# A recurrence step whose first product is cut into column halves of TensorE's array, with part of it summed in the second product's bank

## Chip, cores and metric

The kernel runs on one core of a Trainium2 chip. The metric is the device time of one execution in microseconds (us), the median of several runs. A core has five engines that take their own instructions in order: TensorE (PE; its weight loads are listed as PEld), VectorE (DVE), ScalarE (ACT), GpSimd (POOL) and SyncE (SP, which here issues most DMA transfers). TensorE writes only to PSUM, which has eight banks; GpSimd doesn't read PSUM here.

## What is computed

Two parts. The first is a recurrence over 768 tokens for 4 x 8 heads with a state of 40 x 40 each; the second sends its output through a layer of eight experts. All in f32.

```python
for t in range(S):                                   # S = 768, D = 40
    y[:, :, t] = einsum('bhd,bhde->bhe', rt, state)
    Sa = einsum('bhde,bhe->bhd', state, at)
    state = state * wt[:, :, None, :] - einsum('bhd,bhe->bhde', Sa, bt) \
            + einsum('bhd,bhe->bhde', vt, kt)
...
P = softmax-like weights of x @ w_gate               # x: 3072 x 320, normalised 8 times over rows and columns
for e in range(E):                                   # E = 8, F = 1024
    out += P[:, e:e+1] * (np.maximum(x @ w1[e], 0) @ w2[e])
```

## The kernel before

The recurrence is cut into 12 chunks of 64 tokens (c). In a chunk the tokens' effects on each other are products of small matrices and one triangular inverse, so that only the state goes from chunk to chunk. The 32 heads are four batches (b) of four pairs (p = 0 to 3) of two heads (h = 0, 1). Head 0 of a pair lies on rows 0 to 39, head 1 on rows 64 to 103 of a tile, so a tile has R2 = 104 rows. One step is one (c, b): 48 steps in all.

- `prep(c, b)` makes a step's matrices ahead of it: running products of w (q, g by DVE), scaled k, b and a (kb, ab, mostly by POOL), and from products of those the weights `sx` (104 rows; for each p and h 104 columns: 64 for the chunk's own tokens, then 40 that carry the state and k) and `bb`. It stores g in DRAM (gd).
- `load_lu`, `inv_...`, `finish`, `tload` and `tmat` make the triangular inverses of a group of two chunks and put them together as `tt`; tmat's products are gp (L261) and op (L266), with 64 rows and 64 columns of weights each. gp's operands lie on rows 0 to 63, op's on rows 64 to 127.
- `recur(c, b)` is the step. It loads vz, rb, gl and f, then: av (L289) from r and the state, masked by DVE into f (L290); the first product `xc` (L297), 104 columns of weights from sx times f, one bank for each h; from each bank ACT copies rows 0 to 63 to x1 (L303) and rows 64 to 103 to c1 (L304); pu = tt times x1 (L308), masked by DVE to pm (L310); the second product c2 = bb times pm (L315); DVE adds c1 to it (ws, L317); POOL multiplies columns 0 to 63 by gl to the output y (L321), and columns 64 to 103 by cc to the next state z (L330; in chunks 9 to 10 DVE does that). z is transposed on TensorE (zt, L335) and copied by ACT into vz (L337, L338) and into the next f (L285, L286).
- Every second step stores y to DRAM (xd) and queues a small product lp (`gate`, L345), which `gate_step` hands out one matmul at a time between those of xc.

The four batches are staggered (SKEW) by the list of events at the end of `attention`. That is the order in which the code issues work. The order on each engine is then set by the language's scheduler from its own model of time, up to the eighth block of the experts (N_MAN); behind that it is as written. So a change in one step moves instructions of the whole recurrence on all engines. PSUM tiles of a step come from a pool of four banks (`ps`) that are taken in turn; f has three buffers, gl two, y two, z four.

The experts' part loads and splits weights (`prep_w`) and tokens (`prep_x`), and runs layer1 (L582) and layer2 (L647) with fp32r operands in blocks. Its first blocks are issued behind the recurrence, and the scheduler lets some of their matmuls in between the last steps.

A matmul is given a part of TensorE's 128x128 array by its shape: with 64 columns of weights or fewer half of the array's columns, with 64 rows or fewer half of its rows. Which half follows from the rows on which the output or the operands lie.

Of the kernel before, what the change touches and what calls it, by code (L numbers as in the profile page):

```python
# [11 lines left out]
F32 = mybir.dt.float32  # L12
F32R = mybir.dt.float32r
AF = mybir.ActivationFunctionType
ALU = mybir.AluOpType
# [4 lines left out]
NCH = S // C  # L20
NP = 4
R2 = 104
# [7 lines left out]
def attention(ctx, tc, d, xd, ps, pq, pt, gs, lg):  # L30
    nc = tc.nc
# [3 lines left out]
    const = ctx.enter_context(tc.tile_pool(name="a_const", bufs=1))  # L35
    io = ctx.enter_context(tc.tile_pool(name="a_io", bufs=1))
    wk = ctx.enter_context(tc.tile_pool(name="a_wk", bufs=2))
# [13 lines left out]
    for n in range(NCH * NB - NSX, NCH * NB):  # L51
        i, pool = n % NSX, sets[n - NCH * NB + NSX]
# [12 lines left out]
    lg_b = [const.tile([128, 4 * NP, 64], F32, name="lg")]  # L65
    ab_b = [pin.tile([R2, NP, 128], F32, name=f"ab{i}") for i in range(2)]
    g1_b = [pin.tile([RL, NP, 65], F32, name=f"g1{i}") for i in range(1)]
    vz_b = [const.tile([RL, NP, 104], F32, name=f"vz{i}") for i in range(5)]
    c1_b = [const.tile([R2, NP, 104], F32, name=f"c1{i}") for i in range(2)]
    rb_b = [const.tile([RL, NP, 128], F32, name=f"rb{i}") for i in range(NRB)]  # L70
    y_b = [const.tile([RL, NP, 2, 64], F32, name=f"y{i}") for i in range(2)]
    unf = inv.tile([128, 1056], F32, name="un")
# [14 lines left out]
    def clear():  # L87
        nc.gpsimd.memset(unf, 0.0)
        nc.gpsimd.memset(unf[:, 0:1024:33], 1.0)
        nc.gpsimd.memset(tnf, 0.0)  # L90
        for t in vz_b + rb_b + c1_b + lg_b:
            nc.vector.memset(t, 0.0)
        for t in y_b:
            nc.gpsimd.memset(t[96:RL], 0.0)
        for t in tt_b:
            nc.gpsimd.memset(t, 0.0)
# [6 lines left out]
            nc.scalar.copy(out=sx_b[i][64:R2].rearrange("r p h x -> r (p h) x")[:, :, 64:104],  # L103
                           in_=cst[64:R2, 360:400].unsqueeze(1).broadcast_to([40, 8, 40]))

    state = {"sx": 0, "ab": 0, "g1": 0, "vz": 0, "c1": 0, "t1": 0, "tt": 0, "rb": 0, "y": 0}

    def rot(key, lst):
        i = state[key]
        state[key] = (i + 1) % len(lst)  # L110
        return lst[i]
# [158 lines left out]
    def recur(c, b):  # L270
        pp = preps[c, b]
        vz, zc = vz_cur[b], zp[b]
        nc.sync.dma_start(out=vz[:, :, 0:64], in_=d["v"][c, b])
        rb = rot("rb", rb_b)
        for h in range(2):
            nc.sync.dma_start(out=rb[h * 64:h * 64 + 48, :, h * 64:h * 64 + 64], in_=d["r"][c, b, h])
        gl = io.tile([RL, NP, 65], F32, name="gl", bufs=2)
        nc.sync.dma_start(out=gl.rearrange("r p t -> r (p t)"), in_=pp["g"][:, 0:260])
        f = wk.tile([R2, NP, 2, 104], F32, name="f", bufs=NFB)
        nc.sync.dma_start(out=f[0:64].rearrange("s p h x -> s (p h) x")[:, :, 64:104],  # L280
                          in_=d["vt"][c, b].rearrange("s (g x) -> s g x", x=40))
# [6 lines left out]
        for p in range(NP):  # L288
            nc.tensor.matmul(av[:, p], lhsT=vz[0:R2, p], rhs=rb[0:R2, p], start=True, stop=True)  # L289
        nc.vector.tensor_tensor(  # L290
            out=f[:, :, :, 0:64], in0=av,
            in1=mask_f.unsqueeze(1).unsqueeze(1).broadcast_to([R2, NP, 2, 64]), op=ALU.mult)
        yield
        xc = [ps.tile([R2, NP, 104], F32, name=f"xc{h}", tag="ps") for h in range(2)]
        for h in range(2):
            for p in range(NP):
                nc.tensor.matmul(xc[h][:, p], lhsT=pp["sx"][:, p, h], rhs=f[:, p, h], start=True, stop=True)  # L297
                if p % 2:
                    gate_step()
        x1 = wk.tile([128, NP, 104], F32, name="x1")  # L300
        c1 = rot("c1", c1_b)
        for h in range(2):
            nc.scalar.copy(out=x1[h * 64:h * 64 + 64], in_=xc[h][0:64])  # L303
            nc.scalar.copy(out=c1[h * 64:h * 64 + 40], in_=xc[h][64:104])  # L304
        yield
        pu = ps.tile([128, NP, 104], F32, name="pu", tag="ps")
        for p in range(NP):
            nc.tensor.matmul(pu[:, p], lhsT=tts[c][:, b * NP + p], rhs=x1[:, p], start=True, stop=True)  # L308
        pm = wk.tile([128, NP, 104], F32, name="pm")
        nc.vector.tensor_tensor(out=pm, in0=pu, in1=mask_p.unsqueeze(1).broadcast_to([128, NP, 104]),  # L310
                                op=ALU.mult)
        yield
        c2 = ps.tile([R2, NP, 104], F32, name="c2", tag="ps")
        for p in range(NP):
            nc.tensor.matmul(c2[:, p], lhsT=pp["bb"][:, p], rhs=pm[:, p], start=True, stop=True)  # L315
        ws = wk.tile([R2, NP, 104], F32, name="ws")
        nc.vector.tensor_tensor(out=ws, in0=c2, in1=c1, op=ALU.add)  # L317
        if b % 2 == 0:
            ys[c, b // 2] = rot("y", y_b)
        y = ys[c, b // 2]  # L320
        nc.gpsimd.tensor_tensor(out=y[0:R2, :, b % 2], in0=ws[:, :, 0:64], in1=gl[0:R2, :, 0:64], op=ALU.mult)  # L321
        if b % 2:
            tok = c * 256 + b // 2 * 128
            nc.sync.dma_start(out=xd[0:NP * RL].rearrange("(r p) t -> r p t", p=NP)[:, :, tok:tok + 128],
                              in_=y.rearrange("r p b t -> r p (b t)"))
            gq.append(gate(c, b, y))
        if c + 1 == NCH:
            return
        z = wk.tile([R2, NP, 40], F32, name="z", bufs=4)
        (nc.vector if c >= 9 else nc.gpsimd).tensor_tensor(out=z, in0=ws[:, :, 64:104],  # L330
                                in1=preps[c + 1, b]["cc"].unsqueeze(2).broadcast_to([R2, NP, 40]), op=ALU.mult)
        yield
        zt = ps.tile([40, NP, 104], F32, name="zt", tag="ps")
        for p in range(NP):
# [1 line left out]
        vz = rot("vz", vz_b)  # L336
# [15 lines left out]
    def gate_step():  # L352
        if len(gq) > (GL - 1) // 2:
            next(gq[0])
            gcount[0] += 1
            if gcount[0] % NP == 0:
                gq.popleft()
# [4 lines left out]
    preps, invs, tts = {}, {}, {}  # L362
# [23 lines left out]
    def step(c, b):  # L386
        if (c, b) not in gens:
            gens[c, b] = recur(c, b)
        next(gens[c, b], None)
# [6 lines left out]
    for c in range(NCH):  # L396
# [3 lines left out]
        t = 5 * c + 2 - T_LEAD  # L400
# [3 lines left out]
    for s, cs in enumerate(GROUPS):  # L404
# [3 lines left out]
        for i in range(n):  # L408
            cb = (cs[0] + i // NB, i % NB)
            j = cb[0] * NB + cb[1] - NSX  # L410
            t = 5 * (j // 4) + 3 + SKEW * (j % 4) + 0.01
            t = max(t, t0 + P0[s] + PD * i) if s else -20 + 0.01 * i
# [53 lines left out]
def body(ctx, tc, d, out):  # L466
# [12 lines left out]
    with ExitStack() as actx:  # L479
        ps, pq, pt = (actx.enter_context(tc.tile_pool(name=f"a_ps{i}", bufs=n, space=bass.MemoryType.PSUM))  # L480
                      for i, n in enumerate((PC, PQ, PT)))
        nc.sync.dma_start(out=gs, in_=d["gate"])
        attention(actx, tc, d, xd, ps, pq, pt, gs, lg)
        nc.gpsimd.memset(ones, 1.0)
        nc.sync.dma_start(out=ident, in_=d["cst"][:, 232:360])
# [350 lines left out]
```

## Time and profile before

| | us |
|---|---|
| median of 3 runs | 1834.67 (1831.1 to 1841.27) |
| the profiled execution's own time | 1832.94 |
| its span in the trace | 1831.2 |
| mean granted TensorE clock | 0.959 |

The trace comes from one execution. "Line engine op, out<-in" names a group of instructions by the code's line and the program's tiles; "x" is the count of records. An f32 matmul in the code leaves two records each of weight load and matmul (a transpose leaves one). "Idle before" is time in which the engine stood still ahead of an instruction, with what ended it. In the view by time a matmul's duration contains its way through the array and overlaps the next one, so the pace is read from start to start. "<-" in a view of waits reads: this waited for that.

### The profile page before, as it was taken

The numbers are of one execution on the slowest core, as the hardware profiler recorded it, in microseconds if no ns is written. First come the engines' busy times: TensorE is split into PE (matmuls) and PEld (weight loads), VectorE is DVE, ScalarE is ACT, GpSimd is POOL, SyncE is SP. The second block draws the span as 40 slices with busy tenths as digits, with TensorE's granted clock in tenths as the row PEclk, the third lists the DMA queues.
The fourth block names the chain that finished last, engine by engine and source line by source line (L and its number), as shares of the span: only waits on it lengthen the run. The fifth ranks groups of instructions, "written<-read, shape, count | busy, mean of one in ns | idle before, by whom it ended". The sixth has DMA issues, their size and how long they took to land.

```text
span 1831.2 us, 31655 instructions
## 1 busy us (share of the span) xinstructions
PE 1724.3 (94%) x11843; PEld 1696.8 (93%) x11843; DVE 1365.3 (75%) x2356; ACT 856.8 (47%) x1851; POOL 874.0 (48%) x854
## 2 busy tenths in 40 slices
PE   4479988999989999999999999999999999999999
PEld 4368888898978999999999999999999999999999
DVE  7786996973788867777676878977686877767675
ACT  6347767766743533434343434345343343424342
POOL 6545664723462626447291735008182644628160
PEclk8568988999999999999999999999999999999999
DMA  7468777867520101111020112201020111102001
GB/s 193 116 157 185 175 180 174 186 137 172 152 77 20 57 20 57 38 39 57 20 75 20 57 37 61 69 1 60 16 76 20 57 38 38 57 20 75 15 24 44
DMA packets 211759, 140.47 MB, mean 77 GB/s; under 512 B 162965, under 2 KB 193813, under 8 KB 211605
## 3 DMA queue, kind: packets, MB, share of 16 engines
q1 hardware_dynamic: 207925, 132.70, 27.9%
q10 hardware_dynamic: 3680, 5.74, 1.2%
q8 instruction: 94, 1.54, 0.3%
q14 instruction: 60, 0.49, 0.1%
HBM read 110.78 MB, written 27.61 MB: 76 GB/s over the span
## 4 chain that ended last, share of the span: by engine, by line
PE 75%; DVE 7%; DMA 4%; issue 4%; POOL 3%; ACT 2%; SPq 2%; POOLq 0%; ACTq 0%; DVEq 0%
PE op L647 36%; PE p L582 33%; DMA inp<-in_inp_dram 1%; PE xc L297 1%; PE av L289 1%; PE pu L308 1%; DVE pr L193 1%; DVE hl L606 1%; DVE q L124 1%; PE c L315 1%; DMA ld<-lt 1%; PE op L266 1%; DVE sm L600 1%; PE ll L159 1%; POOL ab L154 1%
## 5 line engine op out<-in xcount | busy, mean ns | idle before, releaser
L582 PE MATMUL p<-xch,wh 128*128 128x384 f32 (+1 forms) x1792 | 605.0, 339 | 8.9 <-DVE sm L600 4.3
L603 ACT ACTIVATE hh<-sm 128x384 fp32r<-128x384 f32 x512 | 269.5, 527 | 728.5 <-DVE sm L600 728.4
L647 PE MATMUL op<-wh,hh 128*128 128x320 f32 x1536 | 477.2, 311 | 4.0 <-ACT hh L603 3.8
L647 PE MATMUL op<-wl,hh 128*128 128x320 f32 x1536 | 474.8, 310 | 0.0
L647 PE MATMUL op<-wh,hl 128*128 128x320 f32 x1536 | 468.0, 309 | 0.9 <-DVE hl L606 0.9
L528 POOL TENSOR_TENSOR wl<-ws,wh 128x640 fp32r<-128x640 f32 x60 | 103.1, 1718 | 606.2 <-ACT wh L526 606.1
L606 DVE SCALAR_TENSOR_TENSOR hl<-sm,hh 128x384 fp32r<-128x384 f32 x512 | 373.1, 762 | 2.6 <-ACT hh L603 1.8
L582 PEld LDWEIGHTS p<-xch,wh 128*128 128x128 f32 (+1 forms) x1792 | 337.0, 188 | 13.3 <-DVE sm L600 5.2
L582 PE MATMUL p<-xcl,wh 128*128 128x384 f32 x896 | 302.3, 337 | 0.0
L582 PE MATMUL p<-xch,wl 128*128 128x384 f32 x896 | 301.8, 337 | 0.0
L647 PEld LDWEIGHTS op<-wh,hh 128*128 128x128 f32 x1536 | 290.2, 189 | 4.9 <-ACT hh L603 4.9
L647 PEld LDWEIGHTS op<-wl,hh 128*128 128x128 f32 x1536 | 291.1, 190 | 0.0
L647 PEld LDWEIGHTS op<-wh,hl 128*128 128x128 f32 x1536 | 286.8, 188 | 1.4 <-DVE hl L606 1.2
L600 DVE TENSOR_TENSOR sm<-p,u 128x384 f32<-128x384 f32 x384 | 236.3, 625 | 8.7
L582 PEld LDWEIGHTS p<-xcl,wh 128*128 128x128 f32 x896 | 168.6, 188 | 0.0
L582 PEld LDWEIGHTS p<-xch,wl 128*128 128x128 f32 x896 | 168.5, 188 | 0.0
L600 DVE TENSOR_TENSOR sm<-p,p 128x384 f32<-128x384 f32 x128 | 71.3, 557 | 129.4 <-PE p L582 75.0
L600 DVE TENSOR_TENSOR p<-p,p 128x384 f32<-128x384 f32 x128 | 71.1, 556 | 101.7 <-PE p L582 101.4
L600 DVE TENSOR_TENSOR u<-p,p 128x384 f32<-128x384 f32 x128 | 70.8, 553 | 57.1 <-PE p L582 55.9
L536 POOL TENSOR_TENSOR wl<-ss,wh 128x512 fp32r<-128x512 f32 x60 | 90.3, 1505 | 28.4 <-ACT wh L533 24.2
L159 PE MATMUL ll<-ab,kb 104*128 104x128 f32 x336 | 62.8, 344 | 40.5 <-POOL kb L147 18.5
L159 PEld LDWEIGHTS ll<-ab,kb 104*128 104x128 f32 x336 | 54.2, 244 | 45.3 <-POOL kb L147 24.8
(163 smaller groups left out, 2727.3 us busy)
## 6 DMA issues: line engine op xcount, KB each, us to landing
ws<-in_wts_dram SPq DMA_DIRECT2D x60, 832.0 KB, 4.5
inp<-in_inp_dram SPq DMA_DIRECT2D x42, 451.5 KB, 4.5
gd<-g SPq DMA_DIRECT2D x48, 113.8 KB, 2.6
gl<-gd SPq DMA_DIRECT2D x48, 113.8 KB, 2.8
vz<-in_v_dram SPq DMA_DIRECT2D x48, 112.0 KB, 3.5
xd<-y SPq DMA_DIRECT2D x24, 224.0 KB, 3.5
ld<-lt ACTq DMA_DIRECT2D x40, 128.0 KB, 2.6
rb<-in_r_dram SPq DMA_DIRECT2D x96, 48.0 KB, 3.1
```

The lines of the kernel that those rows point to most:

```text
L124: nc.vector.tensor_tensor_scan(out=qr.rearrange("r p t -> r (p t)"), data0=w65[:, 260:0:-1], data1=one65, initial=0.0, op0=ALU.mult, op1=A ...
L154: eng.tensor_tensor(out=ab[64:104, :, 64:128], in0=a_in[64:104], in1=g[64:104], op=ALU.mult)
L159: nc.tensor.matmul(ll[:, p], lhsT=kb[:, p], rhs=ab[:, p], start=True, stop=True)
L193: nc.vector.tensor_tensor(out=prv, in0=a.unsqueeze(2).broadcast_to([nu, n_c, n_r, n_k]), in1=m.unsqueeze(1).broadcast_to([nu, n_c, n_r, n_ ...
L266: nc.tensor.matmul(op[:, p], lhsT=gs[:, p], rhs=t2[:, p], start=True, stop=True)
L528: g.tensor_tensor(out=wl[:, 0:640], in0=raw[:, 256:896], in1=wh[:, 0:640], op=ALU.subtract)
L536: g.tensor_tensor(out=lv[:, 3:7], in0=so[:, :, 0], in1=hv[:, 3:7, 0], op=ALU.subtract)
L582: nc.tensor.matmul(o, lhsT=w_, rhs=x_, start=(j == 0), stop=(j == 3))
L600: eng.tensor_tensor(out=out, in0=x, in1=y, op=ALU.add)
L603: nc.scalar.activation(out=hh[:, f, h], in_=sm[f][:, h], func=AF.Relu)
L606: v.scalar_tensor_tensor(out=hl[:, f, h], in0=sm[f][:, h], scalar=0.0, in1=hh[:, f, h], op0=ALU.max, op1=ALU.subtract)
L647: nc.tensor.matmul(ops[i], lhsT=a[:, h, cs], rhs=w_[:, cw], start=(f == 0 and h == 0 and j == 0), stop=(last and h == 1 and j == 2))
```

## The change

The first product no longer uses 104 columns of weights. Its 64 columns go to `xc` alone, head 0 to rows 0 to 63 and head 1 to rows 64 to 127 of one bank, which one ACT copy takes to x1. The 40 columns are separate matmuls that open the sums of the second product's bank: head 0 with a slice of 64 columns that begins at the 40 (the 24 columns behind them land on rows that nothing uses), head 1 with 40. The second product then adds to the same bank, so c1 and ws go. DVE multiplies z and y out of the bank, z first; POOL does neither any more.

```diff
-        xc = [ps.tile([R2, NP, 104], F32, name=f"xc{h}", tag="ps") for h in range(2)]
-        for h in range(2):
-            for p in range(NP):
-                nc.tensor.matmul(xc[h][:, p], lhsT=pp["sx"][:, p, h], rhs=f[:, p, h], start=True, stop=True)
-                if p % 2:
-                    gate_step()
+        xc = ps.tile([128, NP, 104], F32, name="xc", tag="ps")
+        sf = pp["sx"].rearrange("r p h x -> r p (h x)")
+        for p in range(NP):
+            for h in range(2):
+                nc.tensor.matmul(xc[h * 64:h * 64 + 64, p], lhsT=sf[:, p, h * 104:h * 104 + 64], rhs=f[:, p, h],
+                                 start=True, stop=True)
+            gate_step()
         x1 = wk.tile([128, NP, 104], F32, name="x1")
-        c1 = rot("c1", c1_b)
-        for h in range(2):
-            nc.scalar.copy(out=x1[h * 64:h * 64 + 64], in_=xc[h][0:64])
-            nc.scalar.copy(out=c1[h * 64:h * 64 + 40], in_=xc[h][64:104])
+        nc.scalar.copy(out=x1, in_=xc)
...
         for p in range(NP):
-            nc.tensor.matmul(c2[:, p], lhsT=pp["bb"][:, p], rhs=pm[:, p], start=True, stop=True)
-        ws = wk.tile([R2, NP, 104], F32, name="ws")
-        nc.vector.tensor_tensor(out=ws, in0=c2, in1=c1, op=ALU.add)
+            nc.tensor.matmul(c2[0:64, p], lhsT=sf[:, p, 64:128], rhs=f[:, p, 0],
+                             start=(p == 0), stop=False, skip_group_check=True)
+            nc.tensor.matmul(c2[64:104, p], lhsT=sf[:, p, 168:208], rhs=f[:, p, 1],
+                             start=(p == 0), stop=False, skip_group_check=True)
+        for p in range(NP):
+            nc.tensor.matmul(c2[:, p], lhsT=pp["bb"][:, p], rhs=pm[:, p], start=False, stop=True,
+                             skip_group_check=True)
+        if c + 1 < NCH:
+            z = wk.tile([R2, NP, 40], F32, name="z", bufs=4)
+            nc.vector.tensor_tensor(out=z, in0=c2[:, :, 64:104],
+                                    in1=preps[c + 1, b]["cc"].unsqueeze(2).broadcast_to([R2, NP, 40]), op=ALU.mult)
...
-        nc.gpsimd.tensor_tensor(out=y[0:R2, :, b % 2], in0=ws[:, :, 0:64], in1=gl[0:R2, :, 0:64], op=ALU.mult)
+        nc.vector.tensor_tensor(out=y[0:R2, :, b % 2], in0=c2[:, :, 0:64], in1=gl[0:R2, :, 0:64], op=ALU.mult)
...
-        z = wk.tile([R2, NP, 40], F32, name="z", bufs=4)
-        (nc.vector if c >= 9 else nc.gpsimd).tensor_tensor(out=z, in0=ws[:, :, 64:104],
-                                in1=preps[c + 1, b]["cc"].unsqueeze(2).broadcast_to([R2, NP, 40]), op=ALU.mult)
```

The two c1 buffers and their clearing go too. In the rows that follow, "x4" counts matmuls of the code, each of which is two records in the trace; the sizes are output rows and columns. TensorE, one step after the preparations have ended, before:

```order
L335 MATMUL zt<-cst,z 40x104 x4
L315 MATMUL c_4594<-pm,st_185 104x104 x4
L308 MATMUL pu<-x_4545,tt_217 128x104 x4
L297 MATMUL xc_4611<-f,st_187 104x104 x2
L266 MATMUL op<-td,lg 64x32 x8
L297 MATMUL xc_4611<-f,st_187 104x104 x2
L297 MATMUL xc_4612<-f,st_187 104x104 x4
L289 MATMUL av<-rb_232,vz_224 104x128 x4
```

The same place after (the lines have other numbers there: L312 and L314 are the 40 columns, L317 the second product):

```order
L337 MATMUL zt<-cst,z 40x104 x4
L312 MATMUL c_4646<-f,st_185 64x104
L314 MATMUL c_4646<-f,st_185 40x104
L312 MATMUL c_4646<-f,st_185 64x104
L314 MATMUL c_4646<-f,st_185 40x104
L312 MATMUL c_4646<-f,st_185 64x104
L314 MATMUL c_4646<-f,st_185 40x104
L312 MATMUL c_4646<-f,st_185 64x104
L314 MATMUL c_4646<-f,st_185 40x104
L317 MATMUL c_4646<-pm,st_185 104x104 x4
L305 MATMUL pu<-x_4600,tt_217 128x104 x3
L265 MATMUL op<-td,lg 64x32 x8
```

The eight new matmuls stand right ahead of the second product of the same step, behind zt, in alternating halves of the array; op moves from between xc's matmuls to between pu's. On DVE, in the same stretch before:

```order
L310 TENSOR_TENSOR pm<-pu,cst 128x416
L290 TENSOR_TENSOR f<-av,cst 104x8x64
L317 TENSOR_TENSOR ws<-c_4878,c_229 104x416
L330 TENSOR_TENSOR z<-ws,cc_195 104x160
L310 TENSOR_TENSOR pm<-pu,cst 128x416
L290 TENSOR_TENSOR f<-av,cst 104x8x64
```

And after (L321 is z, L326 y, L307 pm, L289 f):

```order
L321 TENSOR_TENSOR z<-c_4702,st_190 104x160
L326 TENSOR_TENSOR y_231<-c_4702,gl 104x4x64
L307 TENSOR_TENSOR pm<-pu,cst 128x416
L351 COPY lg<-lp 128x8
L289 TENSOR_TENSOR f<-av,cst 104x8x64
L321 TENSOR_TENSOR z<-c_4797,st_191 104x160
L326 TENSOR_TENSOR y_232<-c_4797,gl 104x4x64
L307 TENSOR_TENSOR pm<-pu,cst 128x416
```

z and y stand where ws stood, and the next step's pm and f are queued behind y. At the end of the recurrence, TensorE before, with the experts' first matmuls (p, L582) ahead of the last second product:

```order
L308 MATMUL pu<-x_5523,tt_218 128x104 x4
L582 MATMUL p_5786<-xch_5628,wh_5630 128x384
L582 MATMUL p_5786<-xcl_5629,wh_5630 128x384
L582 MATMUL p_5786<-xch_5628,wl_5631 128x384
L582 MATMUL p_5786<-xch_5628,wh_5630 128x384
L582 MATMUL p_5794<-xch_5628,wh_5630 128x384
L582 MATMUL p_5794<-xcl_5629,wh_5630 128x384
L582 MATMUL p_5794<-xch_5628,wl_5631 128x384
L582 MATMUL p_5794<-xch_5628,wh_5630 128x384
L315 MATMUL c_5543<-pm,bb_215 104x104 x4
```

And after:

```order
L347 MATMUL lp<-gs,y_231 128x8
L584 MATMUL p_5827<-xch_5720,wh_5722 128x384
L584 MATMUL p_5827<-xcl_5721,wh_5722 128x384
L584 MATMUL p_5827<-xch_5720,wl_5723 128x384
L584 MATMUL p_5827<-xch_5720,wh_5722 128x384
L584 MATMUL p_5841<-xch_5720,wh_5722 128x384
L584 MATMUL p_5841<-xcl_5721,wh_5722 128x384
L584 MATMUL p_5841<-xch_5720,wl_5723 128x384
L584 MATMUL p_5841<-xch_5720,wh_5722 128x384
L317 MATMUL c_5629<-pm,bb_215 104x104 x4
```

These eight are the only ones of the experts ahead of the last second product after the change; before, twenty more stand between the last four steps.

More of the change, by code (lines that the diff above doesn't have):

```diff
@@ L68, in attention @@
     vz_b = [const.tile([RL, NP, 104], F32, name=f"vz{i}") for i in range(5)]
-    c1_b = [const.tile([R2, NP, 104], F32, name=f"c1{i}") for i in range(2)]
     rb_b = [const.tile([RL, NP, 128], F32, name=f"rb{i}") for i in range(NRB)]
@@ L90, in clear @@
         nc.gpsimd.memset(tnf, 0.0)
-        for t in vz_b + rb_b + c1_b + lg_b:
+        for t in vz_b + rb_b + lg_b:
             nc.vector.memset(t, 0.0)
@@ L104, in first_use @@
                            in_=cst[64:R2, 360:400].unsqueeze(1).broadcast_to([40, 8, 40]))
-    state = {"sx": 0, "ab": 0, "g1": 0, "vz": 0, "c1": 0, "t1": 0, "tt": 0, "rb": 0, "y": 0}
+    state = {"sx": 0, "ab": 0, "g1": 0, "vz": 0, "t1": 0, "tt": 0, "rb": 0, "y": 0}
     def rot(key, lst):
```

## The prediction

> **What bounds the kernel now.** I read the page's busy times first, then the busy time by stage, then TensorE's instructions in order of time, its waits, and last the groups of the other engines. The page's first line of engines and the stages:
>
> ```profile
> PE 1724.3 (94%) x11843; PEld 1696.8 (93%) x11843; DVE 1365.3 (75%) x2356; ACT 856.8 (47%) x1851; POOL 874.0 (48%) x854
> 100.00:384.00 284.00, 251.75 (x2316) 240.94 (x2317) 223.34 (x398) 193.25 (x488) 156.83 (x184) 0.89 0.79 176
> 384.00:484.00 100.00, 95.72 (x945) 91.32 (x943) 61.92 (x108) 67.73 (x162) 35.19 (x42) 0.95 0.70 160
> 484.00:505.00 21.00, 20.43 (x178) 19.79 (x178) 13.91 (x27) 12.51 (x28) 8.45 (x11) 1.00 0.37 110
> 505.00:570.00 65.00, 55.51 (x320) 51.93 (x318) 55.03 (x91) 26.62 (x52) 37.13 (x34) 0.95 0.17 55
> 570.00:1831.00 1261.00, 1253.12 (x7866) 1250.70 (x7866) 933.91 (x1605) 507.12 (x999) 573.27 (x494) 1.00 0.13 42
> ```
>
> A row is one stage in us: its length, then busy time of PE, PEld, DVE, ACT and POOL, then the granted clock. The change touches only the recurrence. That fills 100 to 505 us, with the preparations beside it until 384 us and nearly alone after that. From 570 us the expert layers keep TensorE at 99%, so their length is fixed and the whole time moves by as much as the end of the recurrence moves. From 384 to 505 us TensorE is busy for 116 of 121 us, from 100 to 384 us for 252 of 284: it is the bound, with 32 us of idle in the earlier stage and 5 us in the later.
>
> A busy TensorE is not yet a full one, so I took the pace from start times. TensorE in order of time, at full clock:
>
> ```profile
> 417.33 0.90 PE L297 MATMUL xc<-f,st 104*104 104x104 f32 x8
> 418.16 1.11 PE L266 MATMUL op<-td,lg 64*64 64x32 f32 x16
> 419.21 0.98 PE L297 MATMUL xc<-f,st 104*104 104x104 f32 x8
> 420.02 1.04 PE L289 MATMUL av<-rb,vz 104*104 104x128 f32 x8
> 420.90 0.52 PE L335 MATMUL zt<-cst,z 104*40 104x104 f32 x4
> ...
> 424.21 1.63 PE L297 MATMUL xc<-f,st 104*104 104x104 f32 x16
> 425.68 1.04 PE L289 MATMUL av<-rb,vz 104*104 104x128 f32 x8
> ...
> 427.46 0.53 PE L335 MATMUL zt<-cst,z 104*40 104x104 f32 x4
> 427.83 0.90 PE L315 MATMUL c<-pm,st 128*104 128x104 f32 x8
> 428.57 1.06 PE L308 MATMUL pu<-x,tt 128*128 128x104 f32 x8
> 429.46 0.71 PE L297 MATMUL xc<-f,st 104*104 104x104 f32 x6
> ```
>
> Columns: start, duration, engine and line, output and inputs, rows*columns of weights, rows x columns of the moving operand, records. Each written f32 matmul leaves two records, a transpose one. Nothing idles between these rows. From start to start, xc's 16 records take 425.68 - 424.21 = 1.47 us, 92 ns each, c's eight 0.74 us (92 ns), pu's eight 0.89 us (111 ns), av's eight 0.88 us (110 ns), zt's four 0.37 us (92 ns). pu has 128 columns of weights, av 128 moving ones, and both take 110 ns; xc and c have 104 of each and take 92. zt has only 40 columns of weights and takes 92 too, with 104 moving. So the larger of the two counts sets a record's pace.
>
> **TensorE's share of the change.** A step has 16 records of xc now. It will have 32, 16 for xc and 16 ahead of c in c2, all with 64 or 40 columns of weights and 104 moving. By the zt row narrower weights save nothing: each is 92 ns. In a single line that is 32 x 92 ns = 2.94 us, 1.47 us a step more than now.
>
> But neighbours now sit in different halves of the array's columns (output rows 0 to 63 and 64 to 127), and whether two such streams run side by side decides the case. No row of before has that pair. The nearest is a pair in different halves of the array's rows, at half clock:
>
> ```profile
> 115.03 0.82 PE L266 MATMUL op<-td,lg 64*64 64x32 f32 x6
> 115.56 0.31 PE L261 MATMUL gp<-td,lg 64*64 64x32 f32 x1
> 115.67 0.29 PE L266 MATMUL op<-td,lg 64*64 64x32 f32 x1
> 115.69 0.29 PE L261 MATMUL gp<-td,lg 64*64 64x32 f32 x1
> 115.77 0.29 PE L266 MATMUL op<-td,lg 64*64 64x32 f32 x1
> 115.80 0.29 PE L261 MATMUL gp<-td,lg 64*64 64x32 f32 x1
> 115.88 0.29 PE L266 MATMUL op<-td,lg 64*64 64x32 f32 x1
> ```
>
> op alone goes at 0.107 us a record (115.03 to 115.67, six). Beside gp it still does (115.67, 115.77, 115.88), and gp keeps the same pace between them, 0.02 to 0.03 us behind: two f32 streams with their weight loads, each at full speed. I take the columns to behave like the rows, so the 32 records go as two streams of 16: 1.47 us, the same as now. The bounds are 0 and +1.47 us a step.
>
> The Trainium skill (TensorEngine Tiling (Array Packing), Key Properties) says that different tiles can execute weight loads and matmuls in parallel; the rows above agree for row halves, and nothing in this run shows it for column halves. The same section says that changing the tiling mode drains the engine, which speaks against the change and is the second rival below.
>
> The later stage holds 18 steps and the earlier 30 (pu's records there, 144 and 240, by eight):
>
> ```profile
> L308 PE MATMUL pu<-x,tt 128*128 128x104 f32 x144 | 20.7, 289 | 0.1
> L308 PE MATMUL pu<-x,tt 128*128 128x104 f32 x240 | 35.3, 293 | 4.0 <-ACT x L303 2.8 <-ACT c L304 0.8 <-DVE f L290 0.5
> ```
>
> **The other engines.** Their groups from 100 to 505 us (mean ns behind the busy time; the last row gives min/median/max):
>
> ```profile
> L304 ACT COPY c<-xc 40x416 f32<-40x416 f32 x94 | 47.2, 502 | 2.1 <-DVE ws L317 0.3
> L303 ACT COPY x<-xc 64x416 f32<-64x416 f32 x94 | 46.8, 498 | 27.8 <-PE xc L297 22.3 <-PE gp L261 2.3 <-ACT lt L173 1.6
> L290 DVE TENSOR_TENSOR f<-av,cst 104x512 f32<-104x512 f32 x46 | 31.3, 680 | 26.3 <-PE av L289 26.0
> L317 DVE TENSOR_TENSOR ws<-c,c 104x416 f32<-104x416 f32 x48 | 27.7, 577 | 14.9 <-PE c L315 10.5 <-ACT vz L338 2.2 <-POOL ss L525 1.5
> L321 POOL TENSOR_TENSOR y<-ws,gl 104x256 f32<-104x256 f32 x48 | 39.2, 816 | 99.3 <-DVE ws L317 67.4 <-DVE lg L349 14.6 <-DMA gl<-gd 9.8
> L330 DVE TENSOR_TENSOR z<-ws,cc x8: 316/348/852, 429.6 to 484.1; 104x160 f32<-104x160 f32 x8
> ```
>
> - ACT: four copies of 416 columns, 2 x 502 + 2 x 498 = 2.0 us a step, become one of 128x416. Forty and 64 rows cost the same, so rows don't matter and it takes 0.50. That frees 1.5 us a step, 72 us in all. The stage rows show ACT busy for 193 of 284 us, so this is worth only what TensorE waits for it.
> - DVE: ws (0.577) goes, z and y come, both read from the bank. From 416 to 512 columns the price rises by 0.103 us, 1.07 ns a column, so y (256) costs 0.577 - 0.171 = 0.41 us and z (160) 0.30. In 36 steps that is +0.13 us each, in the eight whose z is on DVE already 0.925 becomes 0.71, and in the last four, without z, 0.577 becomes 0.41: 4.7 - 1.7 - 0.7 = +2 us in all, against 61 us of DVE's idle from 100 to 384 us and 38 us from 384 to 484 us.
> - POOL: y and z leave. y alone is 39 us.
> - y waits for gl's transfer and for a free y buffer. On POOL that held up kb and ab; now f and pm stand behind it on DVE, and TensorE waits for those. The row has 9.8 us of gl; I count it in the upper bound only, as the order puts z, for which zt waits, ahead of y.
>
> What TensorE may get back is in its waits, the first four from 100 to 384 us, the last two from 384 to 505 us (us in total, times, longest):
>
> ```profile
> PE ll L159 <- POOL ab L154: 8.7, 5, 4.1
> PE av L289 <- DVE ws L317: 6.6, 3, 3.1
> PE pu L308 <- ACT x L303: 2.8, 2, 1.5
> PE ll L159 <- POOL kb L147: 2.2, 2, 1.4
> PE gp L261 <- DMA td<-nd: 2.1, 1, 2.1
> PE av L289 <- ACT vz L338: 1.8, 1, 1.8
> ```
>
> The waits for POOL's ab and kb, for ws and for x1 sum to 20 us, and all four producers lose work or go. Part of each is a late input (inp, the inversions) that stays, so I take half, -10 us, with 0 and -22 (the small waits for z and c1 beside them) as ends. After 384 us there is nothing to win: the two waits left are for DMA and for zt.
>
> **The tail.** In the order of before, 28 matmuls of the first expert block stand ahead of the last c; after the change eight do, between the two halves of the last c2. They fill waits of the last steps, which have few neighbours, at the pace of this row:
>
> ```profile
> 501.07 1.42 PE p L582 x8
> ```
>
> It is 0.177 us each, so 20 fewer ahead of the last c cost between 0 and 3.5 us. I take +2, as the shorter path (one copy, no ws) covers part of it. **Sum:** 0 - 10 + 2 = -8 us on the profiled 1832.9 us, which is 1.8 us under the median of the three runs. That gives 1825.
>
> **Rivals.**
>
> *One line (ends slower).* If column halves don't overlap, each step costs 1.47 us more. In the 18 later steps nothing covers it: +26 us. In the 30 earlier ones it is 30 x 1.47 / 0.89 = 49 us, of which TensorE's 32 us of idle can cover from none to all: +17 to +49, middle 33. With the -8 above: 1833 + 26 + 33 - 8 = 1884 (1868 to 1900). A surplus of s us a step costs about (18 + 22) s, so it decides (over 9 us slower) from s = 0.43 on, where 70% or less of the second stream is hidden. For it: no row shows column halves at work, and both streams read the same rows of f. Against: the row halves.
>
> *Changing the array's arrangement costs.* The rows have 417.33 to 418.16 for eight xc (0.83, where 0.74 is their pace) and 419.21 to 420.02 (0.81): 0.08 us into and out of op's 64x64 quarter. In the built program neighbours differ in arrangement at 215 places before and at 366 after, so 151 x 0.08 = +12 us, some 1833 + 12 - 8 = 1837 with the gain, up to 1847 without it. Against: the new places are like av, zt, c, where 420.02 to 420.90 and 427.46 to 427.83 show no gap at all. The drain of the skill's page would be this; the trace agrees for op, not for zt.
>
> *f is held too long (ends slower).* f is read until c2's first matmuls, one more slot of the order than xc; there are three buffers, and the transfer that fills the next f waits for that on SP, with gl, rb and tt queued behind it. Its row (count, size, median us from issue to landing):
>
> ```profile
> f<-in_vt_dram SPq DMA_DIRECT2D x44, 80.0 KB, 3.1
> ```
>
> By the paces above, from that point to the xc that needs the buffer again lie c, pu, xc, av, zt, the 16 and the eight records of the next c2 and the next pu: 0.74 + 0.89 + 0.74 + 0.88 + 0.37 + 0.74 + 0.74 + 0.89 = 6.0 us with two streams, nearly twice 3.1. It decides where landing takes over 6 us; should a third of the 30 earlier steps lose 2 us each, it is +20 and 1845.
>
> *The freed engines matter more.* If all 22 us come back and the tail costs nothing: 1811. For it: five waits for POOL's ab sum to 8.7 us. Against: 67 of POOL's 99 idle us ahead of y only wait for ws.
>
> **How the numbers follow.** Two streams: 0.70, at 1825, its own range 1809 to 1846 (the upper end has 9.8 us of gl and the whole tail, with no gain; the lower one is the last rival, which belongs to it). Of the 0.70, 0.38 lies under 1825.5, 0.29 within 0.5% and 0.03 above. Half a per cent, 9 us, is about what can be told from no change here. Arrangement costs: 0.06, half of it within 0.5%, half above. f held too long: 0.06, two thirds of it above. One line: 0.18, all slower. Together: faster 0.38, same 0.34, slower 0.28. The range runs from 1809 to 1878, which takes in the lower part of the single line.
>
> **What would show it.** Two streams: xc's 16 records, and the 16 ahead of c, in 0.75 to 0.95 us from start to start; one line: 1.4 us or more each. ACT: one copy a step of 0.5 us. DVE: y at 0.4, z at 0.3 us. The stage at 99% would begin 8 us earlier, or some 50 later. Wrong would make me: DVE waiting for gl ahead of f, more idle at the first expert block, or a lower clock between 100 and 384 us than 0.89.

## The result: about one per cent slower, by TensorE's work and in part by its clock

The changed kernel takes 1858.64 us (median of four runs, 1852.36 to 1863.33), the kernel before 1836.1 us beside it: a ratio of 1.012, 95% interval 1.0077 to 1.0164. So it is 22 us slower, where 1825 us, 11 less than these 1836.1, were forecast. A few executions (one each of interleaved, relief_only and the kernel before) ran in a slower state at a lower clock; all ratios, and the means of S and L further down, leave them out. The profiled execution has a span of 1850.6 us (1831.2 before). Its engines over the whole span, from the page of the profile:

```profile
PE 1758.9 (95%) x12611; PEld 1705.0 (92%) x12611; DVE 1358.9 (73%) x2390; ACT 784.5 (42%) x1707; POOL 803.4 (43%) x770
```

ScalarE lost 72 us of work, as the prediction had it, and POOL 71. VectorE lost 6, where 2 more were worked out. TensorE gained 35. The stages (length, then busy time of PE, PEld, DVE, ACT and POOL, then the granted clock):

```profile
100.00:384.00 284.00, 266.68 (x2644) 237.88 (x2643) 214.29 (x415) 144.05 (x386) 105.24 (x124) 0.87 0.76 171
384.00:505.00 121.00, 115.47 (x1358) 103.69 (x1357) 67.62 (x126) 52.15 (x137) 24.72 (x26) 0.96 0.66 153
```

From 100 to 384 us TensorE is now busy for 266.68 us, 14.9 more than before: its idle time there went from 32 to 17 us. But the recurrence doesn't end earlier. TensorE in order of time at the last second product, before (first fence) and after (second):

```profile
502.32 0.89 PE L315 MATMUL c<-pm,bb 128*104 128x104 f32 x8
502.99 0.42 PE L582 MATMUL p<-xch,wh 128*128 128x384 f32 x1
```

```profile
518.45 0.42 PE L584 MATMUL p<-xch,wh 128*128 128x384 f32 x1
...
519.76 0.33 PE L584 MATMUL p<-xch,wh 96*128 96x384 f32 x1
519.93 0.89 PE L317 MATMUL c<-pm,bb 128*104 128x104 f32 x8
520.60 0.42 PE L584 MATMUL p<-xch,wh 128*128 128x384 f32 x1
```

The last c starts at 519.93 us in place of 502.32, 17.6 us later; the span is 19.4 us longer. What is lost is lost ahead of that matmul, inside the recurrence. There, one step in order of time at full clock:

```profile
436.97 0.93 PE L297 MATMUL xc<-f,st 104*64 104x104 f32 x16
437.84 0.39 PE L347 MATMUL lp<-gs,y 104*128 104x8 f32 x2
438.08 1.10 PE L288 MATMUL av<-rb,vz 104*104 104x128 f32 x8
439.11 1.11 PE L260 MATMUL gp<-td,lg 64*64 64x32 f32 x16
440.16 0.54 PE L337 MATMUL zt<-cst,z 104*40 104x104 f32 x4
440.62 0.30 PE L312 MATMUL c<-f,st 104*64 104x104 f32 x1
440.63 0.37 PE L314 MATMUL c<-f,st 104*40 104x104 f32 x2
440.76 0.25 PE L312 MATMUL c<-f,st 104*64 104x104 f32 x1
440.84 0.25 PE L314 MATMUL c<-f,st 104*40 104x104 f32 x1
440.85 0.25 PE L312 MATMUL c<-f,st 104*64 104x104 f32 x1
...
441.30 0.25 PE L312 MATMUL c<-f,st 104*64 104x104 f32 x1
441.48 0.98 PE L317 MATMUL c<-pm,st 128*104 128x104 f32 x8
```

Read the starts. Inside the stretch the 64- and the 40-column records come in pairs, 0.09 us from pair to pair; the starts of the 16 records lie within 0.68 us, 440.62 to 441.30. Two streams do run side by side: one line at 0.09 us a record would need 1.44. The ends of the stretch are dear. Into it: the first record of zt to the first of c takes 0.46 us, where four records need 0.37. Out of it: the stretch takes 0.86 us to the start of the full-array matmul behind it (440.62 to 441.48), where eight pairs at 0.09 need 0.72 (0.05 of the difference lies behind the first pair, 0.09 behind the last), and c's eight records then last 0.98 us where the same eight lasted 0.90 in the row of before (427.83), which is one slow record more. Together 0.09 + 0.14 + 0.08, some 0.3 us for a way in and a way out, of which the kernel before has none around xc and c. Over all such places of this trace at full clock the picture is the same: from the last record of zt to a column half it is 0.183 us (median of 23), in the kernel before from zt to c 0.089 (25). The 64x64 quarters have the same gap in the kernel before: av to gp takes 0.202 us (12), av to zt 0.109 (14). A step has two such stretches now, xc and the part ahead of c, and 33 times the built order puts lp, a full-array matmul, right behind a column half.

### The profile page after: what moved, and what is told of

It reads as the page before. It is cut to its first block, busy times and chain, and to the rows that moved or that the text cites. A ratio compares the mean times of both kernels' runs of the same rounds, so it can differ in the third digit from the quotient of the medians.

```text
span 1850.6 us, 32888 instructions
## 1 busy us (share of the span) xinstructions
PE 1758.9 (95%) x12611; PEld 1705.0 (92%) x12611; DVE 1358.9 (73%) x2390; ACT 784.5 (42%) x1707; POOL 803.4 (43%) x770
## 4 chain that ended last, share of the span: by engine, by line
PE 81%; DVE 6%; DMA 3%; issue 2%; POOL 2%; SPq 2%; ACT 1%; DVEq 0%; POOLq 0%; ACTq 0%
PE op L649 36%; PE p L584 33%; PE c L317 2%; DMA inp<-in_inp_dram 2%; PE pu L305 2%; PE av L288 2%; PE xc L297 1%; PE ll L158 1%; PE c L314 1%; PE gp L260 1%; PE op L265 1%; DVE hl L608 1%; PE lp L347 1%; DVE pr L192 1%; PE zt L337 1%
## 5 line engine op out<-in xcount | busy, mean ns | idle before, releaser
L146 POOL TENSOR_TENSOR kb<-inp,q 104x512 f32<-104x512 f32 x40 | 56.5, 1413 | 103.8 <-DVE q L123 47.9
```

Source lines behind the costliest of these rows:

```text
L146: (nc.gpsimd if cb in KB_POOL else eng).tensor_tensor(out=kb, in0=kb_in, in1=q[0:R2, :, 63::-1].unsqueeze(2).broadcast_to([R2, NP, 2, 64]) ...
```

## The experiments

Two numbers are used throughout. The **changes of arrangement** are counted in the built order: neighbours on TensorE that differ in the part of the array they use (all, a column half, a 64x64 quarter; a transpose counts as all). And each run's span is split by its mean granted clock: **S** = span x clock, **L** = span x (1 - clock), the time that the lower clock took. Between the runs of one kernel S scatters by 2 to 5 us (standard deviation), and much of the difference between runs is in L. The means over the runs of each kernel:

```
kernel             changes  median us  clock   S us    L us
joined_hp            44      1844.34   0.950   1748.7   93.0
split_relief_hp      90      1847.63   0.950   1753.5   91.8
before              144      1834-1838 0.955   1751.9   82.8
relief_only         170      1835.04   0.955   1751.0   82.7
one_hp              206      1853.89   0.947   1753.4   97.8
c_all               239      1854.15   0.951   1762.8   91.5
c_one               254      1839.31   0.955   1757.2   83.0
one_stretch         259      1848.64   0.953   1760.9   86.8
gate_outside        307      1857.40   0.952   1765.5   88.7
after               348      1858.64   0.952   1766.9   89.6
more_f              353      1859.02   0.953   1767.7   87.5
interleaved         639      1942.53   0.925   1793.7  145.0
  streams in series:
c_major             242      1842.20   0.962   1771.4   69.3
h_major             352      1860.42   0.965   1796.2   64.5
  products held together:
joined_crit          46      1938.46   0.920   1781.7  154.1
after_joined_crit   240      1951.47   0.920   1793.8  155.6
```

Over the first twelve, S rises by 0.076 us a change (a straight line through them, correlation 0.97, no kernel more than 5 us off it; 0.063 without the one with 639, at a correlation of 0.92). The last four are left out of it, for reasons told with them. The line rests on the kernels with column halves: the four without them show no clear slope, 1748.7 to 1753.5 us over 44 to 170 changes, though their traces have the 0.09 us at each quarter too. The changed kernel's 204 more are 16 us; its S is 15 us above the kernel before, its L 7 us.

**relief_only: the relief of POOL alone.**

```diff
-        nc.gpsimd.tensor_tensor(out=y[0:R2, :, b % 2], in0=ws[:, :, 0:64], ...
-        (nc.vector if c >= 9 else nc.gpsimd).tensor_tensor(out=z, in0=ws[:, :, 64:104], ...
+            nc.vector.tensor_tensor(out=z, in0=ws[:, :, 64:104], ...
+        nc.vector.tensor_tensor(out=y[0:R2, :, b % 2], in0=ws[:, :, 0:64], ...
```

> Here only the work beside TensorE is changed, against the kernel before: y and z are written by VectorE, from ws, z first; TensorE's instructions and ScalarE's four copies stay. Theory (the changes of the array's arrangement are what costs): what VectorE and POOL do is a relief of the same kind as in the changed kernel, so it ends earlier than before, 1820 to 1832 us against 1836, with fewer waits of TensorE for POOL's ab from 100 to 384 us (8.7 us before). Rival A (y and z on VectorE, and what queues behind them, cost the time): 1842 us or more. Rival B (the idle time of TensorE only shrank because TensorE was slower): 1834 to 1838.

Measured: 1835.04 us, ratio 0.9994 (0.9976 to 1.0012). The gain that the theory gave isn't there, and rival A falls too; rival B holds: no gain and no loss. TensorE's waits from 100 to 384 us:

```profile
PE ll L159 <- POOL ab L154: 7.4, 5, 4.1
PE op L266 <- ACT lg L263: 4.0, 2, 2.3
PE av L289 <- DVE pr L193: 3.0, 1, 3.0
```

The wait for POOL's ab is 7.4 us against 8.7, though y and z are gone from POOL. Of the 8.7 us hardly anything was the doing of y and z.

**gate_outside: lp kept out of xc.**

```diff
-            gate_step()          # inside the loop over p
+        for p in range(NP):      # behind it
+            gate_step()
```

> The changed kernel with the four calls of gate_step behind xc's loop, not inside it. In the built order the changes of arrangement fall from 348 to 307, and the places where lp stands behind a column-half matmul from 33 to 18. Theory: a change costs about 0.13 us (0.09 on the way in, 0.17 on the way out), so 41 fewer save 5 us: 1850 to 1856 against 1858.6. Rival C (lp inside xc is the whole loss): most of the 22 us is regained, 1836 to 1842. Rival D (the scheduler's order or the clock costs the time): no change or a few us either way, with no tie to that count.

Measured: 1857.4 us, ratio to before 1.0108 (1.0085 to 1.0131). Rival C falls. The theory's 5 us are not seen in the time; S fell by 1.4, where 41 changes would give 3.

**one_stretch: one stretch of column halves a step.** The 40-column part moves behind the next batch's xc.

```diff
+        yield                    # between c2's first part and its second
...
+            ev.append((5 * c + (2.15 + SKEW * b if b < 3 else 6.05), step, (c, b)))
```

> The changed kernel with the 40-column matmuls of a step issued right behind the next batch's xc, so that a step has one stretch of column-half matmuls and not two; the bank c2 is held one slot longer, f one slot less. In the built order the changes of arrangement fall from 348 to 259. Theory: 89 x 0.13 = 12 us less, 1843 to 1851 against 1858.6. Rival D (order or clock): 1855 to 1862. Rival E (f held too long): TensorE's waits for rb and f, 7 us in all in the changed kernel, go: 1850 to 1856, with the gaps around column-half matmuls as many and as long as in the changed kernel.

Measured: 1848.64 us, ratio 1.0077 (1.0059 to 1.0095): 10 us under the changed kernel (8 by the two ratios), inside the theory's interval; of rival E's, 1850 to 1856, the time alone doesn't clear it by much, and more_f below speaks to that. S fell by 6.0 for 89 changes (6.8 by the line), L by 2.8.

**more_f: four buffers for f.** `NFB = 3` becomes `NFB = 4`.

> The changed kernel with four buffers for f in place of three; the count of changes is 353 against 348. Rival (f is held too long, and the transfers behind it on SP's queue with it): TensorE's waits for rb, f and y, some 10 us, go: 1846 to 1851. Theory: f's holding has little part in it, at most the 2.3 us of TensorE's wait for f after 384 us: 1855 to 1860.

Measured: 1859.02 us, ratio 1.0104 (1.0081 to 1.0127), no change against the kernel as changed. The rival of f's holding falls.

**interleaved: more changes, the same matmuls.**

```diff
         for p in range(NP):
             nc.tensor.matmul(c2[0:64, p], ...
             nc.tensor.matmul(c2[64:104, p], ...
-        for p in range(NP):
             nc.tensor.matmul(c2[:, p], lhsT=pp["bb"][:, p], rhs=pm[:, p], start=False, stop=True, ...
```

> The changed kernel with the 40-column part taken apart: each pair of 64- and 40-column matmuls stands right ahead of the full-array matmul that adds to the same columns of the bank, so a step has four short stretches of column halves in c2 in place of one. The same matmuls, 639 changes of arrangement in the built order against 348. Theory (the changes are what costs, 0.13 us each by the trace, 0.08 after what idle time and clock give back by the difference of the changed kernel to before): 291 x 0.08 to 0.13 = 23 to 38 us more, 1880 to 1897 against 1858.6. If the price is not in the changes (order, clock, f, y): 1855 to 1863.

Measured: 1942.53 us, ratio 1.0558 (1.0532 to 1.0584): 84 us over the changed kernel, more than twice the most that was expected. TensorE in order of time at full clock:

```profile
442.43 0.30 PE L312 MATMUL c<-f,sx 104*64 104x104 f32 x1
442.44 0.37 PE L314 MATMUL c<-f,sx 104*40 104x104 f32 x2
442.57 0.25 PE L312 MATMUL c<-f,sx 104*64 104x104 f32 x1
442.76 0.43 PE L316 MATMUL c<-pm,bb 128*104 128x104 f32 x2
443.11 0.30 PE L312 MATMUL c<-f,sx 104*64 104x104 f32 x1
```

Six records, four of them in two pairs, take 0.68 us (442.43 to 443.11); at 0.09 us for a pair and for each of c's two they need 0.36. S rises by 26.8 us for 291 changes, 0.092 each, as expected. The rest, 55 us, is L. Stages of this kernel that the clock's steps set off:

```profile
315.00:396.00 81.00, 81.00 (x464) 66.27 (x466) 38.50 (x75) 23.25 (x64) 15.79 (x18) 0.50 0.41 98
397.00:512.00 115.00, 111.81 (x1175) 92.39 (x1173) 67.25 (x124) 47.78 (x128) 25.66 (x30) 1.00 0.66 146
513.00:567.00 54.00, 53.36 (x316) 42.65 (x317) 17.65 (x38) 15.41 (x38) 5.35 (x6) 0.50 0.42 99
```

For 81 us TensorE has a record in flight all the time (81.00 of 81.00) and runs at half clock throughout. Busy in this view is not what the clock goes by.

**joined_crit, after_joined_crit: the 64x64 products held together.**

```diff
-    def tmat(c, half):
-        gl = slice(half * 8, half * 8 + 8)
+    def tmat(c):
+        gl = slice(0, 16)
...
+        with tc.tile_critical():
+            for p in range(4 * NP):
+                nc.tensor.matmul(gp[:, p], ...       # op likewise
```

> The kernel before, with only the 64x64 products gp and op rearranged: the two halves of a chunk in one call, each product's sixteen matmuls held together, so the changes into and out of the array's quarters fall from 144 to 46. No column half anywhere. Theory (any change of arrangement costs, not only those of this edit): 98 x 0.08 to 0.13 = 8 to 13 us less, 1823 to 1828 against 1836. If changes cost only beside column halves, or if the held-together products make others wait: 1833 to 1840 or more.

> The changed kernel with the same rearranged gp and op. The changes fall from 348 to 240. Theory: 108 x 0.08 to 0.13 = 9 to 14 us less, 1845 to 1850 against 1858.6, still above the kernel before. Otherwise as for the kernel before: no change, 1855 to 1863.

Measured: 1938.46 us (ratio 1.0548, 1.0530 to 1.0565) and 1951.47 us (1.0616, 1.0591 to 1.0640). Neither tells anything of the changes. The construction that holds the sixteen together makes their first wait for much that they don't need. Waits from 100 to 384 us of joined_crit:

```profile
PE gp L262 <- DMA gd<-g: 12.9, 3, 5.3
PE gp L262 <- DMA tt<-ud: 4.6, 2, 3.4
PE op L268 <- DMA rb<-in_r_dram: 4.0, 3, 2.6
PE gp L262 <- DVE q L124: 3.9, 1, 3.9
```

**joined_hp: the same without those waits.** `tc.high_priority()` in place of `tc.tile_critical()`, on the kernel before.

> The kernel before with gp and op of a chunk's two halves in one call of sixteen each and written with high priority, without the waits that the held-together version had: 44 changes against 144, no column half anywhere. Theory: 100 x 0.08 to 0.13 = 8 to 13 us less than before, 1823 to 1828. If changes cost only at column halves, or the early sixteen hold up the step's own matmuls: 1833 or more.

Measured: 1844.34 us, ratio 1.0049 (1.0031 to 1.0068): slower by 9 us by the ratio, where 8 to 13 less were expected. S is 3.2 us lower for 100 changes fewer, less than half of the line, and L 10 us higher. The early sixteen put off other work; from 384 to 505 us a single wait stands out:

```profile
PE c L317 <- ACT c L306: 9.7, 1, 9.7
```

**c_one and c_all: column halves in the kernel before, nothing else changed.** c_one writes one of c's four matmuls so, c_all all four.

```diff
-            nc.tensor.matmul(c2[:, p], lhsT=pp["bb"][:, p], rhs=pm[:, p], start=True, stop=True)
+            nc.tensor.matmul(c2[0:64, p], lhsT=pp["bb"][:, p, 0:64], rhs=pm[:, p], start=True, stop=True)
+            nc.tensor.matmul(c2[64:104, p], lhsT=pp["bb"][:, p, 64:104], rhs=pm[:, p], start=True, stop=True)
```

> The kernel before with one matmul of c's four written as two, 64 and 40 columns of the same weights. Nothing else differs: VectorE, POOL and ScalarE do what they did. Each step gets one way into column halves and one out of it; 254 changes in the built order against 144. Theory: 110 x 0.08 to 0.13 = 9 to 14 us more than before, 1845 to 1852, or somewhat more where the granted clock falls as it did with the stretches taken apart. If changes cost nothing by themselves: 1833 to 1841.

> The kernel before with all four matmuls of c written as 64 and 40 columns: 239 changes against 144, nearly as many as with one of them, but four times as many column-half records. Theory (only the ends of a stretch cost; inside it two streams go side by side at 0.68 us for 16 records against 0.74 for the eight now): 95 x 0.08 to 0.13 - 3 = 5 to 9 us more than before, 1841 to 1846, a little under the kernel with one. If the column-half records themselves cost: about four times the loss of the kernel with one.

Measured: c_one 1839.31 us (ratio 1.0037, 1.0010 to 1.0064), c_all 1854.15 us (1.0113, 1.0079 to 1.0147). Column halves alone make the kernel before slower, but the two are the other way round from what the theory said: c_one is below its interval, c_all above. In S they are 5.3 and 10.9 us above before (the line gives 8 and 7), and c_all lost another 9 us to the clock.

**one_hp: one stretch, nothing put between.** one_stretch and gate_outside together, with xc and the 40-column part under high priority.

> The changed kernel with one stretch of column halves a step (the 40-column part behind the next batch's xc), both written with high priority so that the scheduler puts nothing between them, and gate_step behind xc's loop: 206 changes against 348, and lp behind a column half once against 33 times. Theory: 142 x 0.08 to 0.13 = 11 to 18 us less, 1841 to 1848; one kept stretch a step leaves it a few us above the kernel before. Rival (order or f's holding): 1855 to 1862.

Measured: 1853.89 us, ratio 1.0096 (1.0069 to 1.0123), not the 1841 to 1848 expected. S is 1753.4, within 2 us of the kernel before: with 206 changes TensorE's work is nearly back. But L is 97.8, 15 above before. TensorE's waits from 384 to 505 us:

```profile
PE pu L307 <- ACT x L303: 3.7, 1, 3.7
PE xc L298 <- DVE f L289: 2.6, 1, 2.6
```

The stages of a step come in another order now, and single waits of this length are what the kernel before doesn't have there.

**c_major: the same column halves in series.** Whether column halves as such pull the clock down was open here.

```diff
-        for p in range(NP):   # 64 columns, 40 columns, for each p
+        for p in range(NP):   # 64 columns for all four p
+            ...
+        for p in range(NP):   # then 40 columns for all four
```

> The kernel with c in 64 and 40 columns again, but head by head: four 64-column matmuls, then four 40-column ones. As many changes of arrangement (242 against 239) and the same records, only the two streams hardly overlap: the 16 records of a step should take about 1.1 us in place of 0.68, +20 us of TensorE in 48 steps. Theory (the granted clock falls after a 3.4 us window in which records stream for less than about half the time, two side by side counted once): span times (1 - clock), 91.5 us with the pairs, falls to 80 or less, so the time rises by at most 10 us, 1850 to 1865. Rival (column halves pull the clock down because half the array does nothing, or because the step has more records): that number stays at 91 or rises, and the time is 1868 or more.

Measured: 1842.2 us, ratio to before 1.0029 (1.0012 to 1.0046): 12 us faster than c_all (15 by the two ratios), below even the theory's interval. One step of it:

```profile
431.48 0.66 PE L315 MATMUL c<-pm,st 128*64 128x104 f32 x5
431.89 0.28 PE L317 MATMUL c<-pm,st 128*40 128x104 f32 x1
...
432.19 0.61 PE L317 MATMUL c<-pm,st 128*40 128x104 f32 x5
432.73 1.14 PE L308 MATMUL pu<-x,tt 128*128 128x104 f32 x8
```

From 431.48 to 432.73 it is 1.25 us to the next matmul; with the pairs of c_all it was 0.85 (434.48 to 435.33 in its trace). S rises by 8.6 us, and L falls by 22.2. The same stage of c_all (first) and of c_major (second), with the clock as the last column but two:

```profile
100.00:384.00 284.00, 259.54 (x2412) 239.55 (x2412) 219.41 (x379) 187.74 (x473) 150.62 (x180) 0.85 0.78 172
```

```profile
100.00:384.00 284.00, 264.11 (x2547) 243.77 (x2547) 226.04 (x401) 193.72 (x489) 150.82 (x183) 0.92 0.78 175
```

**h_major: the changed kernel with its streams in series.** Its loops run over h outside and p inside; gate_step follows every second p, so lp gets other places too.

> The changed kernel with xc and the 40-column part written head by head: four matmuls into output rows 0 to 63, then four into rows 64 to 127, so that neighbours sit in the same half of the array's columns. The count of changes stays (352 against 348). Theory (the two streams do run side by side): the 16 records of a stretch take about 1.4 us in place of 0.68, two stretches a step, 48 steps: +67 us less what TensorE's 17 idle us cover, 1900 to 1930. Rival (the streams share one line all along, and that is the loss): no change, 1855 to 1862.

Measured: 1860.42 us, ratio 1.0148 (1.0110 to 1.0186), no clear difference from the changed kernel's 1.0120, though TensorE does the serial work that the theory gave it: 1.27 us from xc to av in place of 0.87 from xc to lp above.

```profile
437.56 1.34 PE L297 MATMUL xc<-f,st 104*64 104x104 f32 x16
438.83 1.12 PE L288 MATMUL av<-rb,vz 104*104 104x128 f32 x8
```

S is 29 us higher and L 25 lower. By the time alone this run would say that the two streams are worth nothing; by S they are worth 29 us, and the clock hides it.

**split_relief_hp: a version that might have beaten both.** relief_only with gp and op, eight each, under high priority.

> The kernel before with y and z on VectorE, and gp and op (eight each, as before) written with high priority: 90 changes of arrangement against 144, no column half. Theory (0.08 us a change in span times clock, by the kernels so far): 54 x 0.08 = 4 us less, 1829 to 1833, if the clock stays at 0.955. If the early gp and op open stalls of several us, as the sixteen in one call did, the clock falls and takes it back: 1836 to 1843.

Measured: 1847.63 us, ratio 1.0048 (1.0026 to 1.0069). This is nearest to its second case, and worse than its 1843: S is not lower than before, L is 9 us higher. From 384 to 505 us the early gp and op now wait for 7.7 us, where gp waited for 2.1 before:

```profile
PE gp L262 <- DMA td<-nd: 5.6, 2, 3.2
PE op L268 <- DVE lg L352: 2.1, 1, 2.1
```

No kernel here beats the one before; relief_only equals it.

## Why the prediction was wrong

**TensorE's share, the step that failed.** The prediction put 0 for it: "I take the columns to behave like the rows, so the 32 records go as two streams of 16: 1.47 us, the same as now." Two streams they are: 0.87 and 0.86 us from the start of each 16 to the next matmul, inside the 0.75 to 0.95 that it gave as their mark. What it put at nothing is what stands at their ends: two ways in and out a step, 0.3 us each, less the 0.03 us that 16 pairs at 0.09 save against 1.47, so nearly +0.6 us a step even before lp is put inside xc. Over 48 steps that is an estimated 28 us of TensorE, and with lp's places more. In S it came out as +15 us; TensorE's idle time from 100 to 384 us fell by 15 us at the same time, which would be the rest.

**The rival that was right.** "Changing the array's arrangement costs" had 151 changes at 0.08 us, 1837 to 1847, with a chance of 0.06. The price was near what a change cost in S (0.063 to 0.092 us), in part by luck: in the trace a way in and out costs 0.3 us, 0.15 a change, and the rows that gave 0.08 didn't count the gap behind op's own last record (418.16 to 419.21 is 1.05 us for 16 records, whose pace is 0.058). The idle time that went would be what brings 0.15 down in S. Further, the count was low (204 more, since zt counts as the full array) and the reason against it was wrong. The prediction read av to zt and zt to c as changes without a gap, as if zt's 40 columns of weights were a column half. And its 1837 to 1847 still lie some 12 us or more under the measured 1858.64: its -8 was not there, and it had no term for the clock. That 1858.64 lies inside the stated 1809 to 1878 is luck; the upper part of that range was there for the single line, which the starts refute. In the changed kernel zt to a column half has the gap (0.46 us for 0.37), zt to c had none. A transpose with 40 columns does not leave the full arrangement; it could not speak for 40 columns of a matmul. The drain that the Trainium skill (TensorEngine Tiling (Array Packing), Key Properties) names for a change of tiling mode agrees with the trace, which has 0.09 us on the way in and 0.2 on the way out.

**The relief, -10 us, did not come.** ScalarE's copy took 0.506 us, y 0.412, z 0.312, all as worked out (100 to 505 us):

```profile
L301 ACT COPY x<-xc 128x416 f32<-128x416 f32 x45 | 22.8, 506 | 38.0 <-PE xc L297 32.3 <-DMA inp<-in_inp_dram 2.5 <-PE kt L166 1.4
L326 DVE TENSOR_TENSOR y<-c,gl 104x256 f32<-104x256 f32 x44 | 18.1, 412 | 0.0
L321 DVE TENSOR_TENSOR z<-c,cc 104x160 f32<-104x160 f32 x28 | 8.7, 312 | 17.6 <-PE c L317 17.6
```

relief_only shows that taking y and z from POOL brings nothing (0.9994). The waits for ws, x1 and ab did shrink in the changed kernel, but others stand in their place (100 to 384 us):

```profile
PE av L288 <- DMA rb<-in_r_dram: 4.6, 3, 3.0
PE zt L337 <- DVE y L326: 3.1, 2, 2.1
PE ll L158 <- POOL kb L146: 2.4, 2, 1.4
```

and the idle time of TensorE fell from 32 to 17 us because TensorE itself got slower: the others had more time. c_one and c_all speak for it: they relieve no engine, and TensorE's idle time in that stage falls there too, to 25 and 24 us (258.63 and 259.54 busy). ScalarE's share of the relief was not tried alone.

**The tail, +2 us, held.** The last c came 17.6 us later, the end 19.4: 1.8 us more. That the twenty matmuls are what makes these 1.8 us was not tried.

**f, gl and the single line.** VectorE didn't wait for gl ahead of f, and a fourth f buffer changes nothing. "One line" is refuted by the starts; h_major shows it would have cost 29 us in S.

**The clock.** The prediction counted none of it, and named a lower clock than 0.89 only as a sign of error; it was 0.87. Over the runs it is 7 us of the 22. That pairs lower the clock is shown by c_major and h_major, that gaps do by interleaved; that they are the whole of these 7 us is not.

Open are two things: why c_all is slower than c_one in S at fewer changes, and how much of each kernel's distance to the line is the scheduler's order, which differs a little in all of them.

## What to carry to other kernels

Before narrower matmuls are put into a dense stream, count the changes of the array's arrangement that they add, not only the records they save: here 0.3 us for a way in and out stands against 0.02 us that a stretch of eight pairs saves (0.72 against 0.74). A neighbour that changes arrangement for free must be of the same kind (matmul, not transpose) to prove that the change is free. And split a comparison by the granted clock first: two kernels of the same time here differ by 29 us in S.

## What the hardware showed that was not expected

In these traces the clock goes by how much of the time records stream, not by how busy TensorE looks. In the trace's clock record it steps between 0.5 and 1 in multiples of 3.41 us. I sorted all stretches of 3.41 us from 100 to 505 us of the sixteen traces by the share of time in which a record streams (0.83 ns a moving column, as a record of 128 takes 20 ns more than one of 104, 110 against 90; twice that at half clock; two side by side counted once):

```
clock of a stretch   clock of the next   stretches   median share   best border   rightly told
full                 full                  1258         0.71
full                 half                   138         0.34            0.45           98%
half                 half                   336         0.65
half                 full                   153         0.92            0.84           90%
```

The borders are fitted to these same stretches; to say each time that the clock stays would be right in 90% at full and 69% at half clock. So one stretch under about a half at full clock mostly loses the clock (123 of the 133 below the border), and at half clock it takes a much fuller one to get it back (141 of the 176 above the border do). That fits what the runs did: a wait of some us sends the clock down, and a stream full of gaps, as in interleaved, stays there for 81 us with no wait at all. It also fits c_major and h_major, which do the same work in longer streams and lose less to the clock. The Trainium skill (TensorE: Matmul & The Clock Gate, Part 1: The HAM clock gate) has the 3.4 us window and the two clocks, and this trace agrees; its wording, that an idle window lowers the clock and a busy one raises it, is coarser than what was measured here, where 0.45 and 0.84 are the borders, and the measurement decides.
